# Weight loads in pairs of row pieces and a new instruction order, in four layers of local attention and gated products on one Trainium2 core

## The chip, the core and the metric

The kernel runs on one core of a Trainium2 chip. A core has five engines with a queue of instructions each: TensorE (PE in the profile; its weight loads, which overlap the products, are shown as PEld), VectorE (DVE), ScalarE (ACT), GpSimd (POOL) and SyncE (SP), which here only issues DMA transfers. An engine takes its instructions strictly in order, and each instruction may wait for semaphores that other engines or landed transfers raise. The metric is device time in microseconds; lower is better.

## What is computed

Two layers of attention and two of a gated product, in turn, over 2048 tokens of width 448, all in bfloat16, with the same weights both times:

```python
def _A_ref(x, wqkv, wo):
    H = 16; Dh = D // H
    W, dil = 8, 2
    qkv = (x @ wqkv)
    idx = pos[:, None] - off[None, :]
    logits = jnp.einsum("bhsd,bhswd->bhsw", q, kg) * scale
    attn = _softmax(logits, axis=-1)
    o = jnp.einsum("bhsw,bhswd->bhsd", attn, vg)
    return o @ wo
...
def _B_ref(x, w_gate, w_up, w_down):
    g = jnp.einsum("bsd,df->bsf", x, w_gate)
    u = jnp.einsum("bsd,df->bsf", x, w_up)
    h = g * u
    return jnp.einsum("bsf,fd->bsd", h, w_down)
...
x = x + _A_ref(_layernorm(x), A_wqkv, A_wo)
x = x + _B_ref(_layernorm(x), B_w_gate, B_w_up, B_w_down)
x = x + _A_ref(_layernorm(x), A_wqkv, A_wo)
x = x + _B_ref(_layernorm(x), B_w_gate, B_w_up, B_w_down)
```

Each query looks at 8 keys, 2 tokens apart, backwards. The inner width F of the gated product is 1792. Gate, up and down weights are 1.6 MB each.

## The kernel before

The program is a list of operations with dependencies; a list scheduler in the file (`Sched`, L134 to L522) puts them in order when the program is built, with estimated durations, and writes out one fixed instruction sequence for each engine. An operation's priority is a number for its job plus numbers for its kind (`PR`), for its place in the list (`XP`, some 1,300 entries) and for the job (`JP`). `HEAD_P`, `HOLD_A`, `HOLD_BA`, `HOLD_BB`, `A_CAP`, `B_CAP`, `ATT_P`, `LAND` and `LINE_H` also steer that choice alone. A different number gives a different order, and no other difference.

The tokens are cut into chunks of 256 or 512. A job "A20" is chunk 0 of layer 2, an attention layer; "B10" is chunk 0 of layer 1, a gated product. `SEQ` (L75) interleaves the jobs: `A00 A01 B10 A02 B11 A03 A04 B12 A20` and so on, so that attention work of one layer stands between gated products of another.

- A chunk of attention: normalization on VectorE and ScalarE (L761 to L782: statistics, logarithm and exponential for the root, xn), a transposed copy of xn in `xnTa` (by TensorE in the first layer, by a DMA transpose later), the query and key products (L534, evicted at L892), the value products (evicted at L957 and L984), a copy of some value rows through DRAM (`vt`, L901) that a DMA transpose brings back (L912).
- Attention runs in 9 groups of up to 240 tokens. A group has a score burst of up to 64 small products (L1015), two exponentials on ScalarE (L1024), two masks on VectorE (L1031), a value burst of 64 small products (L1049; AV1, AV2 and so on are the value bursts in the order of time), evictions (L1060, L1064), a shuffle, two passes on ScalarE for the reciprocal (L1074 to L1076), and the product oT (L1087). Then the output projection (L534, `wo_g`) and the add to x (L1104).
- A chunk of the gated product: xn of double width, its DMA transpose into `xnTb` (L785, L786), 14 units of 14 products with `WGU` (L534), each evicted by ScalarE (gate, L1140) and multiplied by VectorE (L1143) into `hT`, and the down products with `WD`.

A product with 64 rows of contraction takes half of the array; the two halves run at the same time, gate weights in partitions 0 to 63 and up weights in 64 to 127 of `WGU`. Small products of the bursts take an eighth each. Inside a burst the scheduler may place strips of a wide product (L537, 32 columns each), so that TensorE has work while its instructions come in.

All loads stand on SP's queue, in its order: x, qkv weights, `wo_g`, a row of ones for `vt`, then the weights of the gated product in six transfers of 784 KB, each waiting for the landing of the one in front: gate half 0, up half 0, gate half 1, up half 1, down half 0, down half 1 (L724 to L729). Behind them on the same queue are the copies to `vt`, the transposes from `vt` and the transposes into `xnTb`. A unit of the gate/up product waits for the gate and up halves that it reads (L1126), a down product for both down transfers.

## Time and profile before

| what | value |
|---|---|
| median of 3 runs | 394.8 us (394.6 to 395.0) |
| profiled execution | 395.59 us |
| its span, first to last instruction | 393.9 us |
| TensorE busy | 381.1 us, 97% |
| VectorE busy | 288.1 us, 73% |
| ScalarE busy | 208.3 us, 53% |
| granted TensorE clock, mean | 0.995 |
| HBM read and written | 8.54 MB, 2.71 MB |

The span runs from the first to the last instruction of the profiled execution; the time of that execution has some 1.7 us around it. A matmul's busy time is modelled to its end, so TensorE is busy also while a short product runs at the pace of its instructions. In stage rows the busy time of each engine stands with its number of instructions; the clock column is the share of full speed that TensorE was granted. In rows of groups a line of the kernel, the engine, the operation, the tiles written and read, the shapes and the count stand ahead of the bar, then the busy time and the mean of one in ns, then the idle time of the engine just before them and what ended it. SPq is SP's DMA queue: the length of a row is that of the issuing, not of the transfer.

### The profile page before, as it was taken

What the parts mean: (1) busy time and instruction counts of PE and PEld (TensorE: products, weight loads), DVE (VectorE), ACT (ScalarE), POOL (GpSimd) and SP (SyncE); (2) the same over time, 40 slices, a digit from 0 to 9 for tenths busy, and PEclk for the clock granted to TensorE, in tenths of its full rate; (3) what the DMA queues carried; (4) which work ended last, traced back from release to release, by engine and by line L of the source; (5) the groups of instructions that cost most, each with busy time, mean ns of one, the idle gap of its engine ahead of it and who ended that gap; (6) DMA issues with size and microseconds to landing.
All of it is one profiled execution on the core that took longest, in us unless ns stands there. A gap on an engine that the chain in (4) does not pass through costs nothing.

```text
span 393.9 us, 14839 instructions
## 1 busy us (share of the span) xinstructions
PE 381.1 (97%) x6577; PEld 214.8 (55%) x6577; DVE 288.1 (73%) x637; ACT 208.3 (53%) x392; POOL 8.8 (2%) x39
## 2 busy tenths in 40 slices
PE   8987879999999999999999999999999999999997
PEld 3644447755555454544575666755455445544764
DVE  6996787989995986598454997658978776766432
ACT  4887677757761665454445555445655543434410
POOL 7010000000000000000000000000000000000000
PEclk9999998999999999999999999999999999999999
DMA  8474663311331052301204022510314020304001
GB/s 277 128 154 91 165 147 48 60 38 24 41 63 25 17 77 52 37 2 36 44 17 60 3 41 51 82 33 27 54 26 73 25 47 3 96 1 49 2 25 48
DMA packets 54708, 22.53 MB, mean 57 GB/s; under 512 B 44837, under 2 KB 54645, under 8 KB 54645
## 3 DMA queue, kind: packets, MB, share of 16 engines
q1 hardware_dynamic: 54212, 21.07, 27.0%
q8 instruction: 52, 0.85, 0.9%
q10 hardware_dynamic: 432, 0.52, 0.5%
q14 instruction: 12, 0.09, 0.1%
HBM read 8.54 MB, written 2.71 MB: 29 GB/s over the span
## 4 chain that ended last, share of the span: by engine, by line
PE 86%; ACT 4%; DVE 4%; DMA 3%; issue 2%; SPq 1%
PE ps L534 77%; PE ps L537 3%; PE ps L1049 2%; PE ps L1015 2%; DMA x_sb<-in_A_x_dram 2%; PE ps L1155 1%; ACT qk L892 1%; ACT R_sb L1075 1%; SPq L627 1%; ACT E_sb L1024 1%; DMA xnTb<-xn_sb 1%; DVE hT L1143 1%; DVE x_sb L1104 1%; ACT R_sb L1076 1%; DVE st L761 1%
## 5 line engine op out<-in xcount | busy, mean ns | idle before, releaser
L534 PE MATMUL ps<-xnTb,WGU 64*128 64x512 bf16 (+1 forms) x1932 | 177.5, 335 | 2.3 <-DMA xnTb<-xn_sb 2.3
L534 PEld LDWEIGHTS ps<-xnTb,WGU 64*128 64x128 bf16 x1932 | 94.2, 94 | 76.4 <-issue 4.0
L1140 ACT ACTIVATE g_sb<-ps 128x512 bf16<-128x512 f32 (+1 forms) x140 | 71.5, 511 | 97.8 <-PE ps L534 79.1
L1143 DVE TENSOR_TENSOR hT<-g_sb,ps 128x512 bf16<-128x512 bf16 (+1 forms) x140 | 80.1, 577 | 47.8 <-ACT g_sb L1140 46.0
L534 PE MATMUL ps<-WD,hT 64*128 64x448 bf16 x760 | 77.6, 349 | 0.0
L534 PE MATMUL ps<-xnTa,WQK 64*128 64x512 bf16 (+1 forms) x492 | 53.5, 352 | 0.6 <-DVE hT L1143 0.4
L534 PEld LDWEIGHTS ps<-WD,hT 64*128 64x128 bf16 x760 | 35.8, 94 | 31.6
L1024 ACT ACTIVATE E_sb<-ps,shift_sb 128x1024 bf16<-128x1024 f32 (+1 forms) x36 | 36.8, 1071 | 20.5 <-PE ps L1015 20.4
L1104 DVE TENSOR_TENSOR x_sb<-x_sb,ps 128x448 bf16<-128x448 bf16 x62 | 36.0, 617 | 12.9 <-PE ps L534 12.7
L761 DVE BATCH_NORM_STATS2 st<-x_sb 128x6 f32<-128x448 bf16 x64 | 37.5, 615 | 0.1
L782 DVE TENSOR_SCALAR xn_sb<-x_sb,mv,rstd 128x896 bf16<-128x896 bf16 (+1 forms) x64 | 34.5, 570 | 3.2 <-ACT rstd L766 2.0
L534 PEld LDWEIGHTS ps<-xnTa,WQK 64*128 64x128 bf16 x492 | 24.2, 94 | 20.5 <-DVE hT L1143 0.8
L1031 DVE TENSOR_TENSOR E_sb<-E_sb,MK 128x1024 bf16<-128x1024 bf16 (+1 forms) x36 | 23.6, 664 | 11.1 <-ACT E_sb L1024 10.8
L534 PE MATMUL ps<-wo_g,oT 64*128 64x448 bf16 x252 | 29.2, 349 | 0.1
L892 ACT ACTIVATE qk<-ps 128x1024 bf16<-128x1024 f32 (+1 forms) x24 | 21.8, 917 | 12.8 <-PE ps L534 12.6
L1075 ACT ACTIVATE R_sb<-R_sb 128x480 f32<-128x480 f32 (+1 forms) x34 | 20.5, 603 | 8.0 <-DVE R_sb L1074 7.7
L1087 DVE TENSOR_TENSOR oT<-O_sb,R_sb 128x480 bf16<-128x480 f32 (+3 forms) x36 | 21.9, 628 | 2.7 <-ACT R_sb L1076 2.5
L1060 ACT ACTIVATE O_sb<-ps 128x448 f32<-128x448 f32 (+3 forms) x27 | 14.1, 553 | 18.0 <-PE ps L1049 17.9
L1074 DVE STREAM_SHUFFLE R_sb<-O_sb 128x480 f32<-128x480 f32 (+1 forms) x34 | 22.8, 696 | 0.0
L534 PE MATMUL ps<-WV,xnTa 64*128 64x336 bf16 (+3 forms) x242 | 22.5, 303 | 0.0
L892 DVE CAST qk<-ps 128x1024 bf16<-128x1024 f32 (+1 forms) x12 | 13.6, 1133 | 11.9 <-PE ps L534 11.9
L1076 ACT ACTIVATE R_sb<-R_sb 128x480 f32<-128x480 f32 (+1 forms) x34 | 19.8, 598 | 0.3
(66 smaller groups left out, 233.0 us busy)
## 6 DMA issues: line engine op xcount, KB each, us to landing
out_dram<-x_sb SPq DMA_DIRECT2D x15, 112.0 KB, 1.7
WGU<-in_B_w_gate_dram SPq DMA_DIRECT2D x2, 784.0 KB, 6.8
WGU<-in_B_w_up_dram SPq DMA_DIRECT2D x2, 784.0 KB, 6.6
WD<-in_B_w_down_dram SPq DMA_DIRECT2D x2, 784.0 KB, 4.8
x_sb<-in_A_x_dram SPq DMA_DIRECT2D x3, 448.0 KB, 6.0
vt<-qk SPq DMA_DIRECT2D x42, 16.0 KB
xnTb<-xn_sb SPq DMA_TRANSPOSE x32, 3.1
x_sb<-in_A_x_dram SPq DMA_DIRECT2D x2, 224.0 KB, 4.6
```

Source lines behind the costliest of these rows:

```text
L534: return lambda E: E.matmul(out(), lhs(), rhs(), start=start, stop=stop)
L761: sc.add("dve", one(lambda E, B=B: E.bn_stats(st6[:, B, :], x_sb[:, B, :]), ("bn", li, B)), 525.0, deps=[("x", li - 1, B)] + ([("xn", li - ...
L782: sc.add("dve", one(lambda E, B=B, dst=dst, src=src: E.tensor_scalar(dst, src, mv[:, B, 0:1], rstd[:, B:B + 1], ALU.subtract, ALU.mult), ( ...
L892: return E.activation(dst, src, ACT.Copy) if hasattr(E, "activation") else E.tensor_copy(dst, src)
L1024: return E.activation(E_sb[:, slot, 2 * hp:2 * hp + 2, 0:w], ps[:, b0:b0 + 2, 0:w], ACT.Exp, bias=shift_sb[:, 0:1], scale=SCALE)
L1031: return E.tensor_tensor(e, e, MK[:, kind, 0:nc].unsqueeze(1).unsqueeze(1).to_broadcast([128, 2, w // nc, nc]), ALU.min)
L1074: sc.add("dve", one(lambda E: E.stream_shuffle(R_sb[:, rs, 0:w], O_sb[:, os_, 0:w], [DH] * 32), ("Rs", li, qb)), dve_est(w) + 20.0, deps=[ ...
L1075: sc.add("act", one(lambda E: E.activation(R_sb[:, rs, 0:w], R_sb[:, rs, 0:w], ACT.Ln), ("Rl", li, qb)), act_est(w, False), deps=[("Rs", l ...
L1076: sc.add("act", one(lambda E: E.activation(R_sb[:, rs, 0:w], R_sb[:, rs, 0:w], ACT.Exp, scale=-1.0), ("R", li, qb)), act_est(w, False), de ...
L1104: sc.add("dve", one(lambda E: E.tensor_tensor(x_sb[:, B, :], x_sb[:, B, :], ps[:, bk[w], 0:D], ALU.add), ("x", li, B)), dve_est(D), deps=[ ...
L1140: sc.add("act", one(lambda E, gs=gs, bk=bk: E.activation(g_sb[:, gs, 0:nt], ps[:, bk[0], 0:nt], ACT.Copy), ("G", li, j, fc)), act_est(nt), ...
L1143: sc.add("dve", one(lambda E, gs=gs, bk=bk, fc=fc: E.tensor_tensor(hT[:, fc, hs, 0:nt], g_sb[:, gs, 0:nt], ps[:, bk[1], 0:nt], ALU.mult), ...
```

## The change

The loads of the gated product's weights are cut differently. For each half of F there are three pieces of rows (`KPARTS`: 2, 2 and 3 of the 7 row blocks of 64); the gate piece and the up piece are issued together, and the next pair waits for both to land. The down weights come in four pieces of 3, 4, 3 and 4 row blocks, each waiting for the piece in front. Pieces of one half share a semaphore, with a count for each (the scheduler's `mode`). A unit of the gate/up product waits for all three pieces of its half, a down product for all four. The transfer of ones waits for the four `wo` transfers as before.

All the numbers of the scheduler are new (`PR`, `XP`, `JP`, `HEAD_P`, the holds, `LAND`, `LINE_H`, `ATT_P`, `A_CAP`, `B_CAP`), so every engine's order is new. The instructions are the same but for the loads and the number of strips: 6565 products on TensorE instead of 6577. On SP's queue the first copies to `vt` stand between the fifth and the sixth pair, and two transposes into `xnTb` stand ahead of the first down piece; the fourth down piece stands behind a third one. On TensorE 999 products stand ahead of the first gate/up product instead of 935, among them the third value burst, and the first fourteen gate/up units have no burst between them.

```diff
-HEAD_P = (-2835.6, -2749.66, 4208.49, 2014.49, -243.09)
-HOLD_A = 5030.0
-HOLD_BA = 1290.0
-HOLD_BB = 620.0
+HEAD_P = (-7243.45, -6839.28, 6873.65, 2231.18, -2220.8)
+HOLD_A = 5940.0
+HOLD_BA = 13780.0
+HOLD_BB = 680.0
...
+KPARTS = ((0, 2), (2, 4), (4, 7))
...
-ATT_P = 6.0
-A_CAP = 6
-B_CAP = 8
+ATT_P = 3.0
+A_CAP = 5
+B_CAP = 6
...
-    LINE_H = 9300.0
+    LINE_H = 6500.0
...
-    def plain_dma(q, dst, src, key, sem, deps=(), lat=LOAD_L, prio=0.0, tmin=None):
+    def plain_dma(q, dst, src, key, sem, deps=(), lat=LOAD_L, prio=0.0, tmin=None, mode=0):
...
+    gate = [("wo", j) for j in range(4)]
     for n in range(2):
         f0, f1 = F // 2 * n, F // 2 * (n + 1)
-        plain_dma("sp", WGU[64:128, :, f0:f1], B_w_up[:, f0:f1].rearrange("(k p) f -> p k f", p=64), ("wu", n), f"d_wu{n}", deps=[("wg", n)], lat=LOAD_L + 784 / RATE, prio=-44)
-        plain_dma("sp", WGU[0:64, :, f0:f1], B_w_gate[:, f0:f1].rearrange("(k p) f -> p k f", p=64), ("wg", n), f"d_wg{n}", deps=[("wu", 0) if n else ("wo", 3)], lat=LOAD_L + 784 / RATE, prio=-44)
-    for n in range(2):
-        plain_dma("sp", WD[:, 7 * n:7 * n + 7, :], B_w_down[F // 2 * n:F // 2 * n + F // 2, :].rearrange("(c p) e -> p c e", p=128), ("wd", n), f"d_wd{n}", deps=[("wd", 0) if n else ("wu", 1)], lat=LOAD_L + 784 / RATE, prio=-44)
-    WDR = [("wd", 0), ("wd", 1)]
+        for i, (a, z) in enumerate(KPARTS):
+            for w, lo, src in (("wg", 0, B_w_gate), ("wu", 64, B_w_up)):
+                plain_dma("sp", WGU[lo:lo + 64, a:z, f0:f1], src[64 * a:64 * z, f0:f1].rearrange("(k p) f -> p k f", p=64), (w, n, i), f"d_{w}{n}", deps=gate, lat=LOAD_L + 224 * (z - a) / RATE, prio=-44, mode=i)
+            gate = [("wg", n, i), ("wu", n, i)]
+    for n in range(FC // 7 * 2):
+        a, z = 7 * n // 2, 7 * (n + 1) // 2
+        plain_dma("sp", WD[:, a:z, :], B_w_down[128 * a:128 * z, :].rearrange("(c p) e -> p c e", p=128), ("wd", n), f"d_wd{n // 2}", deps=gate, lat=LOAD_L + 112 * (z - a) / RATE, prio=-44, mode=n % 2)
+        gate = [("wd", n)]
+    WDR = [("wd", n) for n in range(4)]
...
-            return dict(bk=acq, out=out, n=nt, deps=[(w, n) for w in ("wg", "wu") for n in range(1 + (128 * fc + 128 > F // 2))],
+            return dict(bk=acq, out=out, n=nt, deps=[(w, n, i) for w in ("wg", "wu") for n in range(1 + (128 * fc + 128 > F // 2)) for i in range(len(KPARTS))],
```

More of the change, by code (lines that the diff above doesn't have):

```diff
@@ L61 @@
-JP = {'A20': -697.04, 'B32': -598.99, 'B34': -1387.93, 'A22': 1516.07, 'B13': 3108.07, 'A21': -1307.14, 'B12': -64.59, 'A02': 125.15, 'A03': 770.84, 'B30': 3086.52, 'B31': -1192.52, 'B10': -1995.52, 'B11': -915.69, 'A23': -3947.09, 'A04': -1459.04, 'B33': -501.93, 'A01': -1029.7, 'B14': -665.97, 'A00': 1187.84}
+PR = {'Qz': 1078.85, 'AV': -4851.85, 'rstd': -1339.07, 'bn': 4568.65, 'N': -1817.78, 'Gps': 8610.65, 'Tps': -31.38, 'H': -4889.6, 'S': 2643.48, 'VT': 544.99, 'Ex': 596.45, 'G': -2837.24, 'xn': -3500.95, 'QK': 2639.1, 'Ddps': 940.66, 'V': 567.07, 'x': -8.65, 'lnv': 5266.82, 'Oc': 2625.17, 'Oa': 3443.2, 'R': -727.31, 'VVps': -3592.23, 'Yps': -11164.33, 'PW': 3164.05, 'T': -1396.37, 'mv': -2211.6, 'Rs': 1799.38, 'Rl': -488.18, 'QKps': 1399.61, 'E': 778.94, 'wqk': 1537.92, 'wqp': 1028.96}
@@ L62 @@
+JP = {'A20': -25.69, 'B32': -196.33, 'B34': -5191.89, 'A22': -98.13, 'B13': 6648.45, 'A21': -2562.96, 'B12': 1135.93, 'A02': 1939.91, 'A03': 1924.97, 'B30': 4558.29, 'B31': -653.55, 'B10': -3350.57, 'B11': -1722.9, 'A23': -7569.63, 'A04': -2325.27, 'B33': 4017.0, 'A01': -2467.87, 'B14': -3725.84, 'A00': -900.45}
 LOAD_L = 2000.0
-LAND = {"x0": 3800.0, "x0h": 6250.0, "x1": 7450.0, "x2": 10100.0, "x3": 12350.0, "stg0": 3700.0, "stg2": 4900.0, "stg1": 5050.0, "stg3": 5650.0, "wv": 8850.0, "stv": 10550.0}
+LAND = {"x0": 3850.0, "x0h": 6700.0, "x1": 7950.0, "x2": 10600.0, "x3": 12050.0, "stg0": 3500.0, "stg2": 4800.0, "stg1": 5100.0, "stg3": 5650.0, "wv": 9300.0, "stv": 11000.0}
@@ L624, in act_table_load @@
         return E.add_instruction(atl)
-    def plain_dma(q, dst, src, key, sem, deps=(), lat=LOAD_L, prio=0.0, tmin=None):
-        sc.add(q, one(lambda E: E.dma_start(dst, src), key), {"sp": 520.0, "act": 500.0, "pool": 1000.0}[q], deps=deps, dma=sem, mode=0, lat=lat, land=LAND.get(sem[2:], 0.0), prio=prio, tmin=tmin)
+    def plain_dma(q, dst, src, key, sem, deps=(), lat=LOAD_L, prio=0.0, tmin=None, mode=0):
+        sc.add(q, one(lambda E: E.dma_start(dst, src), key), {"sp": 520.0, "act": 500.0, "pool": 1000.0}[q], deps=deps, dma=sem, mode=mode, lat=lat, land=LAND.get(sem[2:], 0.0), prio=prio, tmin=tmin)
     CH_ROWS = [0, 128, 192, 320]
@@ L718, in build @@
     ones_src = ones32[0:32, :].unsqueeze(1).to_broadcast([32, 16, 128])
-    plain_dma("sp", ones_dst, ones_src, ("vones",), "d_one", deps=["c_ones", ("wo", 3)], lat=8000.0, prio=-44.5)
+    plain_dma("sp", ones_dst, ones_src, ("vones",), "d_one", deps=["c_ones"] + [("wo", j) for j in range(4)], lat=4000.0, prio=-44.5)
     for j in range(4):
@@ L722, in build @@
         src = A_wo.rearrange("(c j e) d -> j e c d", c=4, j=4, e=DH)[j]
-        plain_dma("sp", dst, src, ("wo", j), "d_wo", deps=["c_wo", ("x", -1, 11)], lat=LOAD_L + 98 / RATE, prio=-45)
+        plain_dma("sp", dst, src, ("wo", j), "d_wo", deps=["c_wo", ("x", -1, 11)], lat=3600.0, prio=-45)
+    gate = [("wo", j) for j in range(4)]
     for n in range(2):
         f0, f1 = F // 2 * n, F // 2 * (n + 1)
-        plain_dma("sp", WGU[64:128, :, f0:f1], B_w_up[:, f0:f1].rearrange("(k p) f -> p k f", p=64), ("wu", n), f"d_wu{n}", deps=[("wg", n)], lat=LOAD_L + 784 / RATE, prio=-44)
-        plain_dma("sp", WGU[0:64, :, f0:f1], B_w_gate[:, f0:f1].rearrange("(k p) f -> p k f", p=64), ("wg", n), f"d_wg{n}", deps=[("wu", 0) if n else ("wo", 3)], lat=LOAD_L + 784 / RATE, prio=-44)
-    for n in range(2):
-        plain_dma("sp", WD[:, 7 * n:7 * n + 7, :], B_w_down[F // 2 * n:F // 2 * n + F // 2, :].rearrange("(c p) e -> p c e", p=128), ("wd", n), f"d_wd{n}", deps=[("wd", 0) if n else ("wu", 1)], lat=LOAD_L + 784 / RATE, prio=-44)
-    WDR = [("wd", 0), ("wd", 1)]
+        for i, (a, z) in enumerate(KPARTS):
[7 more added lines that the diff above has]
+    WDR = [("wd", n) for n in range(4)]
     WO = [("wo", j) for j in range(4)]
```

3 lines of the change are left out of this document (1 added, 2 removed).

## The prediction

> **What bounds the kernel now.** I read the page first, then the stages, then TensorE's waits, then the queue that issues the loads.
>
> ```profile
> span 393.9 us, 14839 instructions
> ...
> q8 instruction: 52, 0.85, 0.9%
> ```
>
> The profiled execution took 395.59 us: the span and 1.7 us around it. The runs shown have a median of 394.8, so this execution is 0.8 above them; I add my sum to the median.
>
> Stages (length, then busy us and instruction counts of PE, PEld, DVE, ACT, POOL, then granted clock, DMA share, GB/s):
>
> ```profile
> 0.00:58.36 58.36, 48.66 (x935) 27.27 (x936) 48.03 (x127) 41.35 (x77) 8.75 (x39) 1.00 0.64 162
> 25.80:32.70 6.90, 5.23 (x127) 2.68 (x128) 5.08 (x13) 4.88 (x6) 0.00 (x0) 1.00 0.66 128
> 32.70:39.19 6.49, 6.08 (x127) 3.86 (x127) 4.96 (x10) 5.60 (x11) 0.00 (x0) 1.00 0.57 118
> 58.36:76.31 17.95, 17.95 (x468) 13.75 (x470) 14.09 (x38) 12.73 (x30) 0.00 (x0) 0.90 0.34 49
> 58.98:62.39 3.41, 3.41 (x112) 2.35 (x110) 0.79 (x3) 1.68 (x4) 0.00 (x0) 0.50 0.17 29
> 76.31:391.30 314.99, 314.46 (x5178) 173.81 (x5173) 225.64 (x473) 154.19 (x286) 0.00 (x0) 1.00 0.22 38
> ```
>
> From 76.31 us on TensorE is busy 314.46 of 314.99 us while VectorE has 28% to spare: an order can gain next to nothing there. Ahead of it lie 9.7 us of idle TensorE (58.36 less 48.66) and a stretch of 3.41 us at clock 0.50, which costs half its length, **1.7 us**. All that this change can win is in these first 76 us. TensorE's waits:
>
> ```profile
> PE ps L1049 <- issue: 3.3, 2, 1.7
> PE ps L534 <- DMA xnTb<-xn_sb: 2.3, 1, 2.3
> ...
> PE ps L1015 <- issue: 1.0, 2, 0.6
> ```
>
> "Issue" means that TensorE waited for nothing the profile shows. These four stalls, **4.3 us**, end at 25.80, 32.70, 39.19 and 45.84, and the stage rows say what they are: exactly 127 matmuls lie between one end and the next. The page has 52 packets in the instruction queue for 6577 matmuls and as many weight loads: one packet holds some 253 instructions, the 127 matmuls with their loads. TensorE stands at the end of a piece of its program and waits for the next. The load queue gives the beat (start, length of the issue):
>
> ```profile
> 17.45 0.71 SPq L627 DMA_DIRECT2D WGU<-in_B_w_gate_dram  x1
> 24.23 0.59 SPq L627 DMA_DIRECT2D WGU<-in_B_w_up_dram  x1
> ...
> 49.39 4.33 SPq L901 DMA_DIRECT2D vt<-qk  x12
> 53.76 2.68 SPq L785 DMA_TRANSPOSE xnTb<-xn_sb  x2
> ```
>
> The weight loads follow each other every 6.8 us (17.45 to 24.23), and the stalls end every 6.9, 6.5 and 6.7 us. I read it so: an instruction packet stands behind the whole weight transfer in flight. The last two rows explain the wait of 2.3 us: the transposes that the first gate/up product reads stand on the same queue, behind all six weight loads and twelve copies.
>
> ```profile
> 45.84 0.70 PE ps L1049 x59
> ...
> 55.16 2.96 DMA xnTb<-xn_sb
> ```
>
> So the second attention group's value products (AV2) end at 46.5 us, the first gate/up product starts at 58.36.
>
> **The change part by part.** *Loads.* Six transfers of 784 KB become twelve of 224 or 336 KB in six pairs, then four down pieces of 336 or 448 KB, in the same rows and bytes.
>
> ```profile
> out_dram<-x_sb SPq DMA_DIRECT2D x15, 112.0 KB, 1.7
> WGU<-in_B_w_gate_dram SPq DMA_DIRECT2D x2, 784.0 KB, 6.8
> WGU<-in_B_w_up_dram SPq DMA_DIRECT2D x2, 784.0 KB, 6.6
> WD<-in_B_w_down_dram SPq DMA_DIRECT2D x2, 784.0 KB, 4.8
> ```
>
> No row shows a pair. Between 112 KB in 1.7 us and 784 KB in 6.8 us, in proportion, a pair of 448 KB takes 4.2 us and one of 672 KB 5.9; by the down row's 4.8 us it is 3.3 and 4.3; at worst each step costs 6.8. I take the dearer proportion, since both halves write 64 partitions as the gate does: six pairs 28.6 us, landed at 17.45 + 28.6, with a delay behind seven copies **at about 46.6 us**. Down pieces come to 2.7 and 3.3 us. Ten more issues of about 0.6 us put 6 us on SP's queue. Behind its waits stand the copies to vt, the value transposes and the xnTb transposes; in the new order two xnTb transposes stand ahead of all down pieces, and the fourth down piece stands behind a transpose that waits for VectorE.
>
> *Instruction stalls.* A packet now waits for a pair's stream, at most 5.9 us and mostly under 4.2, with a gap after each. The bounds are 4.3 us gained and none. What they covered comes forward: the attention chain. Its prices:
>
> ```profile
> L1024 ACT ACTIVATE E_sb<-ps,shift_sb 128x1024 bf16<-128x1024 f32 x32 | 34.0, 1112 | 20.5 <-PE ps L1015 20.4
> ...
> L1143 DVE TENSOR_TENSOR hT<-g_sb,ps 128x256 bf16<-128x256 bf16 x56 | 23.1, 418 | 18.4 <-ACT g_sb L1140 17.9 <-PE ps L534 0.5
> L782 DVE TENSOR_SCALAR xn_sb<-x_sb,mv,rstd 128x896 bf16<-128x896 bf16 x32 | 22.9, 735 | 2.3 <-ACT rstd L766 1.4 <-DMA xnTa<-xn_sb 0.9
> L1031 DVE TENSOR_TENSOR E_sb<-E_sb,MK 128x1024 bf16<-128x1024 bf16 x32 | 21.9, 690 | 11.1 <-ACT E_sb L1024 10.8
> L1140 ACT ACTIVATE g_sb<-ps 128x256 bf16<-128x256 f32 x56 | 21.4, 384 | 34.8 <-PE ps L534 24.3 <-DVE hT L1143 9.5 <-DVE mv L763 0.8
> L1074 DVE STREAM_SHUFFLE R_sb<-O_sb 128x480 f32<-128x480 f32 x32 | 21.4, 695 | 0.0
> L1087 DVE TENSOR_TENSOR oT<-O_sb,R_sb 128x480 bf16<-128x480 f32 x30 | 19.3, 655 | 2.7 <-ACT R_sb L1076 2.5
> L1075 ACT ACTIVATE R_sb<-R_sb 128x480 f32<-128x480 f32 x32 | 19.2, 601 | 5.9 <-DVE R_sb L1074 5.5
> L1076 ACT ACTIVATE R_sb<-R_sb 128x480 f32<-128x480 f32 x32 | 18.6, 596 | 0.3
> L892 ACT ACTIVATE qk<-ps 128x1024 bf16<-128x1024 f32 x18 | 18.4, 1025 | 11.7 <-PE ps L534 11.5
> ```
>
> In the new order the second half of AV1 waits for two exponentials (2.2 us), a copy out of PSUM half an eviction long (0.6) and an eviction (1.0) after the second score burst. That burst waits for the same vector work as before and ends just after 25.80 again: 29.8, and AV1, 1.1 us long, ends at 31.0. Eleven vector operations (three shuffles, two oT products, an eviction, two v copies, three small ones) then take 7.2 us to the third score burst; that burst, a reciprocal, an eviction, two exponentials and a mask take 4.2, AV2 itself 1.1. **AV2 ends at 43.5 us, 3.0 earlier**, at the same amount of TensorE work done. So 1.3 of the 4.3 us goes back to ACT and VectorE.
>
> *The wait for xnTb.* After AV2 the new order puts the fourth score burst and AV3 ahead of the first gate/up product. VectorE reaches the second xn at AV2 + 4.5; SP then has three copies (0.36 each by the row of twelve) and the transpose (1.34, and 3.0 to its landing), which is down at AV2 + 9.3. TensorE gets to that product only at AV2 + 11.6, because AV3 waits for a mask that ACT's two reciprocals (four passes of 0.6), two evictions and two exponentials precede. Before it was 11.9. The wait for DMA is hidden, a wait of 1.1 us for the mask takes its place; with 0.2 us more streaming and one burst more done by then this is **0.9 us won**. The product starts at 55.1.
>
> *Clock.* The half-clock stage starts 0.6 us after the idle of 2.3 us and takes 1.7 us. The two waits of 1.6 and 1.7 us had none behind them. I count it as caused by the longer idle and gone with it: **1.7 us**; the bounds are 0 and 1.7.
> [...]
>
> *First down projection.* The spacing of TensorE's work:
>
> ```profile
> 75.56 0.94 PE L534 MATMUL ps<-xnTb,WGU 64*128 64x256 bf16 x14
> 76.31 1.50 PE L534 MATMUL ps<-WD,hT 64*128 64x448 bf16 x14
> ```
>
> A unit of 14 matmuls of 256 columns takes 0.75 us; other widths I take in proportion. By the count of the order, streaming up to the first down product is 56.9 us before and 55.4 after. The new order runs all fourteen gate/up units without a score or value burst between them. VectorE must put out 14 products (5.9 us), four adds and four statistics (5.2 at the 0.65 of the other 448 to 480 wide operations), three xn (2.2), two shuffles and two oT (2.7): 16.0 us, of which 1 us falls ahead of the stretch, against 13.2 us of streaming. I walk to 15.0 us from the first gate/up product to the first down product; before it was 17.95 with 1.7 of half clock, 14.9 of streaming and three bursts: 0.1 of waiting. **1.7 us lost** (bounds 0.5 and 2.5). The first down product is then at 70.1 us.
>
> *Down weights.* The fourth piece is issued after the transpose of the third xn, at about 65.2, and lands by 68.9: 1.2 us to spare. So nothing.
>
> *The rest.* Streaming is the same, 361.4 us in all. A burst costs 0.4 us beside its streaming (76.31 to the end: 315 us for 304.5 of streaming and 25 bursts); there are 33 runs of bursts instead of 34: **0.4 us won**. Constants, estimates and semaphore modes make no instruction of their own. The order behind 76 us I count at 0, bounds 1 won and 2 lost: nothing spare covers it.
>
> Sum: -3.0 - 0.9 - 1.7 + 1.7 - 0.4 = **-4.3 us, 390.5 us**.
>
> **The rivals.** [...] 0.12. [...]
> *Instruction packets still wait*: pairs fill the queue as a single load did, 1.0 instead of 3.0 is won: 392.5. For: two requests may meet a 672 KB pair. 0.13.
> *The lead is given back* to VectorE behind the first down product: about 394.4. For: it is busy 14.09 of 17.95 us there; against: its 28% idle after 76.31. 0.10.
> *Slower*: a step costs 6.7 us whatever its size. Six pairs end at 17.45 + 40.2 = 57.7, just in time for the fourth gate/up unit, which needs the second half; four down pieces of 4.8 end at 76.9, 6.8 us after TensorE wants them, and an idle that long brings 1.7 of half clock: 390.5 + 8.5 = 399.0. It decides once the last piece lands over 2.6 us late. For: ten landings in a row instead of six, the last behind a transpose; against: 112 KB land in 1.7 us. The change would then not do what it says. 0.11.
>
> **How the numbers follow.** The forecast holds 0.50 (389.5 to 391.8), a gain beyond it, down to 388.8 where the gate/up run loses nothing, 0.04. A measurement tells 0.2%, 0.8 us, from no change. Faster: 0.50 + 0.04 + 0.12 + 0.13 and 0.04 of the third rival, 0.83; same 0.06; slower 0.11. The range 388.8 to 393.9 takes in the first two rivals and most of the third.
>
> **What would show it.** Right: TensorE's issue waits under 1.5 us in all; no wait for xnTb; no 0.50 clock between 50 and 70 us; first gate/up product near 55, first down product near 70; copies of the gate loads on SP's queue every 4 to 6 us. Wrong: a TensorE wait for WGU or WD, a half-clock stage, or a sum of TensorE waits behind 76 us above 2 us.

## The result, and the profile after

The changed kernel takes 390.69 us (median of 15 runs, 388.63 to 394.44) beside 394.84 for the kernel before (15 runs, 393.19 to 396.09) on the same chip: a ratio of 0.9899, 95% interval 0.9873 to 0.9925. The forecast was 390.5. Its profiled execution took 391.56 us with a span of 389.6. All lines of the kernel from the first table on stand a little lower: L534 is now L535, L1015 is L1021, L1024 is L1030, L1049 is L1055, L1143 is L1149, L785 is L791.

TensorE's waits in the changed kernel (total, times, longest, in us):

```profile
PE ps L535 <- DMA WD<-in_B_w_down_dram: 1.4, 1, 1.4
PE ps L697 <- DVE eps_sb L658: 1.3, 1, 1.3
PE ps L1021 <- issue: 1.2, 1, 1.2
PE ps L802 <- DVE WQK L713: 0.7, 1, 0.7
PE ps L1021 <- ACT xnTa L812: 0.6, 1, 0.6
PE ps L535 <- ACT E_sb L1030: 0.3, 1, 0.3
```

The wait of 2.3 us for xnTb is gone, and of 4.3 us of issue stalls one of 1.2 us is left. A wait of 1.4 us for the down weights is new. The same stages as before, then the half-clock stage (length, busy us and counts of PE, PEld, DVE, ACT, POOL, granted clock, DMA share, GB/s):

```profile
0.00:55.62 55.62, 51.00 (x999) 28.39 (x1000) 46.83 (x125) 41.08 (x79) 7.83 (x37) 0.97 0.60 147
55.62:70.48 14.86, 13.45 (x227) 12.04 (x228) 14.16 (x36) 9.15 (x25) 0.00 (x0) 1.00 0.55 134
...
70.48:387.00 316.52, 316.26 (x5340) 174.25 (x5340) 225.59 (x477) 158.81 (x290) 0.00 (x0) 1.00 0.22 39
26.64:30.05 3.41, 3.41 (x34) 2.11 (x30) 2.02 (x4) 2.30 (x4) 0.00 (x0) 0.50 0.83 186
```

TensorE's idle time ahead of the first gate/up product falls from 9.70 to 4.62 us, the stretch to the first down product has 1.41 us of idle where it had none, and what follows has 0.26 instead of 0.53. That is 3.94 us less idle. Busy time up to the end of these stages falls by 0.36. Together 4.30 us, which is all of the shorter span. The half-clock stage is still there. It has moved from 58.98 to 26.64.

The chain of waits (start, length, what) shows the milestones:

```profile
43.72 0.09 PE ps L1055 x19
43.80 4.79 PE ps L535 x52
48.59 0.22 PE ps L1021 x16
48.81 1.22 issue
...
55.62 8.60 PE ps L535 x148
...
66.43 3.96 DMA WD<-in_B_w_down_dram
...
70.48 1.50 PE ps L535 x14
```

| milestone, us | before | forecast | after |
|---|---|---|---|
| AV2 ends | 46.5 | 43.5 | 43.8 |
| first gate/up product | 58.36 | 55.1 | 55.62 |
| first down product | 76.31 | 70.1 | 70.48 |

The milestones move from one execution to the next. The first matmuls of 512 columns start 0.43 us apart until the clock is full and 0.215 us apart from there on, and that moment comes at 4.36 us in the profile of before, at 6.16 in this one and at 4.89 in a second profile of the changed kernel, which has its milestones at 43.0, 53.70 and 68.66. By the spacing, the 1.8 us between the first two cost the changed kernel some 0.9 us in this comparison (an estimate); the clock column does not count that stretch.

The queue that issues the loads (start, length of the issue):

```profile
16.37 0.70 SPq L628 DMA_DIRECT2D WGU<-in_B_w_gate_dram  x1
...
21.03 0.60 SPq L628 DMA_DIRECT2D WGU<-in_B_w_gate_dram  x1
...
65.10 1.28 SPq L791 DMA_TRANSPOSE xnTb<-xn_sb  x1
66.43 0.58 SPq L628 DMA_DIRECT2D WD<-in_B_w_down_dram  x1
```

The first two pairs, 448 KB each, are 4.66 us apart, where single loads of 784 KB were 6.8 apart: pieces do land in less time, as assumed. All six pairs take longer than forecast: the last one lands at 49.61 and not at about 46.6, which costs nothing, since the first gate/up product starts at 55.62. The fourth down piece is issued at 66.43, behind a transpose for which VectorE had to finish, and TensorE wants it at 69.1.

### The profile page after: what moved, and what is told of

Its sections match the earlier page's. It is cut to its first block, busy times and chain, and to the rows that moved or that the text cites. A ratio compares the mean times of both kernels' runs of the same rounds, so it can differ in the third digit from the quotient of the medians.

```text
span 389.6 us, 14816 instructions
## 1 busy us (share of the span) xinstructions
PE 380.8 (98%) x6565; PEld 214.7 (55%) x6565; DVE 287.0 (74%) x638; ACT 209.0 (54%) x393; POOL 7.8 (2%) x37
## 4 chain that ended last, share of the span: by engine, by line
PE 93%; ACT 3%; DMA 1%; issue 1%; DVE 1%; SPq 0%; ACTq 0%
PE ps L535 82%; PE ps L538 3%; PE ps L1055 2%; PE ps L1021 2%; PE ps L697 2%; ACT E_sb L1030 1%; PE ps L1161 1%; DMA WD<-in_B_w_down_dram 1%; ACT xnTa L812 1%; ACT qk L898 1%; ACT g_sb L1146 0%; ACT xnTa L809 0%; DVE x_sb L1110 0%; PE ps L802 0%; DVE hT L1149 0%
## 5 line engine op out<-in xcount | busy, mean ns | idle before, releaser
L535 PE MATMUL ps<-xnTb,WGU 64*128 64x512 bf16 (+1 forms) x1908 | 174.4, 332 | 0.2
L535 PEld LDWEIGHTS ps<-xnTb,WGU 64*128 64x128 bf16 x1908 | 92.6, 94 | 67.8 <-issue 1.1
L1149 DVE TENSOR_TENSOR hT<-g_sb,ps 128x512 bf16<-128x512 bf16 (+1 forms) x140 | 79.6, 576 | 43.1 <-ACT g_sb L1146 40.7
L535 PE MATMUL ps<-WD,hT 64*128 64x448 bf16 x778 | 78.6, 349 | 1.5 <-DMA WD<-in_B_w_down_dram 1.4
L535 PEld LDWEIGHTS ps<-WD,hT 64*128 64x128 bf16 x778 | 36.9, 94 | 36.0 <-issue 1.7
L535 PE MATMUL ps<-xnTa,WQK 64*128 64x512 bf16 (+1 forms) x492 | 55.2, 360 | 0.5 <-ACT E_sb L1030 0.3
L1030 ACT ACTIVATE E_sb<-ps,shift_sb 128x1024 bf16<-128x1024 f32 (+1 forms) x36 | 36.8, 1073 | 24.5 <-PE ps L1021 24.4
L535 PEld LDWEIGHTS ps<-xnTa,WQK 64*128 64x128 bf16 x492 | 23.9, 96 | 22.2 <-issue 1.5
L898 ACT ACTIVATE qk<-ps 128x1024 bf16<-128x1024 f32 (+1 forms) x26 | 24.6, 956 | 11.3 <-PE ps L535 11.2
L535 PE MATMUL ps<-wo_g,oT 64*128 64x448 bf16 x256 | 29.1, 349 | 0.1
L535 PE MATMUL ps<-WV,xnTa 64*128 64x336 bf16 (+3 forms) x248 | 23.1, 304 | 0.0
L1009 DVE TENSOR_SCALAR Qz<-qk,qmask 128x960 bf16<-128x960 bf16 (+1 forms) x36 | 14.7, 451 | 9.2 <-PE ps L1021 8.0
L535 PEld LDWEIGHTS ps<-wo_g,oT 64*128 64x128 bf16 x256 | 12.4, 94 | 12.4 <-DVE oT L1093 0.9
```

The lines of the kernel that those rows point to most:

```text
L535: return lambda E: E.matmul(out(), lhs(), rhs(), start=start, stop=stop)
L898: return E.activation(dst, src, ACT.Copy) if hasattr(E, "activation") else E.tensor_copy(dst, src)
L1030: return E.activation(E_sb[:, slot, 2 * hp:2 * hp + 2, 0:w], ps[:, b0:b0 + 2, 0:w], ACT.Exp, bias=shift_sb[:, 0:1], scale=SCALE)
L1149: sc.add("dve", one(lambda E, gs=gs, bk=bk, fc=fc: E.tensor_tensor(hT[:, fc, hs, 0:nt], g_sb[:, gs, 0:nt], ps[:, bk[1], 0:nt], ALU.mult), ...
```

## The experiments

The questions were: is it the pieces or the order that takes the stalls away; is a packet of instructions really behind the transfer in flight; what brings the half-clock stage; and what the late down piece costs. In the diffs that move something on SP's queue, `SPQ` is that queue after the scheduler has run, so that no other engine's order changes. The last four runs were made on one chip, with a median of 394.31 us for the kernel before; the first four beside 394.66, the second four beside 395.16.

### The new order with whole loads

```diff
+            o.ins = [(lambda E, n=n, f0=f0, f1=f1, lo=lo, src=src: E.dma_start(WGU[lo:lo + 64, :, f0:f1], src[:, f0:f1].rearrange("(k p) f -> p k f", p=64)), (w, n, 0))]
+            o.deps = [("wg", n, 0)] if w == "wu" else [("wu", 0, 0)] if n else [("wo", j) for j in range(4)]
+            for i in (1, 2):
+                SPQ.pop(at((w, n, i)))
...
+        o.ins = [(lambda E, n=n: E.dma_start(WD[:, 7 * n:7 * n + 7, :], B_w_down[F // 2 * n:F // 2 * n + F // 2, :].rearrange("(c p) e -> p c e", p=128)), ("wd", 2 * n))]
+        SPQ.pop(at(("wd", 2 * n + 1)))
```

> The new order with the six whole loads of before, each on the landing of the one in front. Theory (an instruction packet stands behind the weight transfer in flight, so small pieces took the stalls away): TensorE's issue waits come back, 3 to 4 us in the first 55 us instead of 1.2, at a beat of 6.5 to 6.9 us; the wait of 1.4 us for WD goes, since the second down load is issued where piece three was (57 to 61 us) and lands by 66. Sum 390.7 + 2.5 - 1.4 = 391.8 us (391 to 393). Rival (the order alone took the stalls away): issue waits stay near 1.2 us, WD wait gone, 389.3 us.

390.35 us (4 runs, 389.72 to 392.12), ratio 0.9904, 0.9877 to 0.9931: as fast as the changed kernel. Its chain and its load queue:

```profile
24.92 0.41 issue
25.33 0.24 PE ps L1021 x2
...
31.23 0.92 issue
32.16 0.23 PE ps L1055 x9
...
43.66 1.50 issue
45.17 0.27 PE ps L1055 x20
```

```profile
23.77 0.60 SPq L1245 DMA_DIRECT2D WGU<-in_B_w_up_dram  x1
30.39 0.60 SPq L1245 DMA_DIRECT2D WGU<-in_B_w_gate_dram  x1
...
59.93 0.41 SPq L1251 DMA_DIRECT2D WD<-in_B_w_down_dram  x1
```

With whole loads three stalls of 2.8 us in all are back, each ending some 1.6 to 1.8 us after a load gave way to the next (25.33 after 23.77, 32.16 after 30.39; the third, 45.17, stands 1.6 us behind the landing of the fourth load at 43.58). The trace also has the instruction packets themselves, on queue q8, 16 KB each. Those that TensorE waits for here end at 24.07, 30.55 and 43.88, each 0.2 to 0.3 us behind the landing of a load, and TensorE goes on 1.3 to 1.6 us after each. In the profile of the kernel before such packets end at 24.50, 31.09, 37.66 and 44.50, 0.1 to 0.3 us behind the landings of the first four loads, and TensorE goes on 1.3 to 1.6 us after each. The theory of the stalls holds. But the time does not rise by the 2.5 less 1.4 us expected: this order starts its last down load at 59.93, and there is no wait for WD at all. The stalls came out smaller than the expected 3 to 4, and the two sums cancel.

The same two kernels once more, side by side:

> The new order with the six whole loads, again. If the pieces gain in issue stalls what they give back in the wait for WD: within 0.6 us of the changed kernel, with issue stalls of 2.4 to 2.8 us and no wait for WD. Rival (the pieces are worth a gain of their own that the first run missed): 1 us or more above the changed kernel.

> The changed kernel again, beside the next two on one chip. 390.7 us, waits of 1.2 us for instructions and 1.4 us for WD.

Whole loads 390.21 us (6 runs, ratio 0.9879, 0.9853 to 0.9906), the changed kernel 390.16 (6 runs, 0.9881, 0.9855 to 0.9908), with 2.8 us of issue stalls and no wait for WD in the first and 0.2 of stalls and 1.5 of WD in the second. **In the new order the cutting of the loads shows no gain (each ratio is known to some 1 us either way); the whole 4.1 us come with the order.** The first profile with whole loads says how. Its first gate/up product starts at 56.44, and TensorE is idle for 5.95 us ahead of it instead of 9.70: the issue stalls are 1.5 us less than in the kernel before, and the wait of 2.25 us for xnTb is gone.

### Uncut pairs

```diff
+            o.ins = [(lambda E, n=n, f0=f0, f1=f1, lo=lo, src=src: E.dma_start(WGU[lo:lo + 64, :, f0:f1], src[:, f0:f1].rearrange("(k p) f -> p k f", p=64)), (w, n, 0))]
+            for i in (1, 2):
+                SPQ.pop(at((w, n, i)))
```

> The changed kernel with gate and up of each half issued together but uncut: two pairs of 1568 KB in flight instead of six of 448 and 672. Theory (packets wait for what is in flight): a pair streams for some 10 to 13 us, so a packet that is asked for early in it comes up to 8 us late; issue waits of 4 to 10 us in all, time 393 to 398 us. Rival (issuing both halves together is what helped, not the size in flight): issue waits near 1.2 us, 390.7 us.

393.13 us (10 runs, ratio 0.9969, 0.9948 to 0.999). Load queue, then chain:

```profile
18.43 0.62 SPq L1245 DMA_DIRECT2D WGU<-in_B_w_up_dram  x1
28.94 0.59 SPq L1245 DMA_DIRECT2D WGU<-in_B_w_gate_dram  x1
```

```profile
24.09 0.66 PE ps L1021 x50
24.76 4.10 issue
28.85 0.24 PE ps L1021 x2
```

The stall starts where it did with whole loads (24.92 there) but lasts 4.10 us instead of 0.41. That it ends where the next pair is issued, 28.85 against 28.94, looks like a wait for the whole pair, but the packet's own record speaks against it. From 25.7 to 27.2 us the DMA queues (packets, MB, share of the 16 engines' time) show the packet among those of the load:

```profile
q1 hardware_dynamic: 134, 0.22, 79.2%
q8 instruction: 1, 0.02, 5.7%
```

It runs from 25.80 to 27.17, behind the gate load, which landed at 24.89, and ahead of the end of the up load, which landed at 28.88; TensorE goes on 1.7 us after it. In the four stalls of the kernel before that was 1.3 to 1.6 us, and in the one of the changed kernel 1.5 (the packet ended at 48.50, TensorE goes on at 50.03). With whole loads the same packet ended 3.1 us earlier, at 24.07. So with 1568 KB in flight TensorE stood longer than with 784 KB (4.10 us for 0.41), but the packet did not wait for all of it. The second pair hit nothing that waited.

### The old order with the new pieces

```diff
+    for key, fn, total in ((("wg", 0), s_g0, 48), (("wu", 0), s_u0, 48), (("wg", 1), s_g1, 48), (("wu", 1), s_u1, 48), (("wd", 0), s_d0, 32), (("wd", 1), s_d1, 32)):
+        SPQ[i] = ([o], [(o, fn)])
```

Each `s_` function waits for the piece in front and issues one pair (the fourth place three pairs, a down place two pieces).

> The old order on all engines, with the pieces in the old six places of SP's queue (pairs in the gate and up places, two down pieces in each down place). Theory: issue waits shrink from 4.3 us to 1 to 2 us, but ten landings instead of five stand in front of the copies to vt and the xnTb transposes, so these come 4 to 8 us later than at 53.76 us and the wait for xnTb grows from 2.3 to some 7 us: 396 to 400 us, slower than before. Rival (loads alone bring the gain): 391 to 392 us.

405.71 us (4 runs, ratio 1.0298, 1.0264 to 1.0333). A wait of TensorE and the rows of the queue behind it:

```profile
PE ps L535 <- DMA xnTb<-xn_sb: 10.2, 1, 10.2
```

```profile
54.68 3.33 SPq L1246 DMA_DIRECT2D WD<-in_B_w_down_dram  x2
58.05 4.25 SPq L902 DMA_DIRECT2D vt<-qk  x12
62.35 2.68 SPq L786 DMA_TRANSPOSE xnTb<-xn_sb  x2
```

The direction was expected, the size was not (7 us of wait, 396 to 400 us), and the issue stalls are 3.4 us, not 1 to 2. The transposes come 8.6 us later than at 53.76, and the clock is halved from 61.9 to 72.2 us, around and behind that idle. In the second form the down places were moved behind the transposes, the first of them by

```diff
+    move(("wd", 0), ("T", 1, 1))
+    move(("wd", 1), ("VT", 0, 7))
```

> As the run with the old order and the new pieces, but the first two down pieces stand behind the first two xnTb transposes and the other two behind a later value transpose. Theory: issue waits 1 to 2 us instead of 4.3, and the wait for xnTb shrinks under 1 us as the transposes no longer wait for down weights; ACT and VectorE take back about 1.3 us: 391 to 392.5 us. Rival (only the whole new order can use the pieces, since the old one's queues wait elsewhere): 394 to 395 us.

396.27 us (4 runs, ratio 1.0048, 1.0031 to 1.0064), slower than before.

```profile
PE ps L535 <- DMA xnTb<-xn_sb: 3.2, 1, 3.2
PE ps L1016 <- issue: 1.5, 1, 1.5
```

```profile
48.47 1.34 SPq L786 DMA_TRANSPOSE xnTb<-xn_sb  x1
49.91 3.39 SPq L1246 DMA_DIRECT2D WD<-in_B_w_down_dram  x2
53.35 1.22 SPq L786 DMA_TRANSPOSE xnTb<-xn_sb  x1
```

The issue stalls ahead of the first gate/up product are 1.5 us; in the first form, with the same load queue up to 46 us, they were 3.4. The packets came alike: the second of them ended at 32.20 there and at 31.91 here. But here TensorE ran at half clock from 26.58 to 29.99, so it wanted that packet at 33.22 and not at 31.85, and did not have to wait. A smaller sum of stalls is thus not by itself a gain. The edit put the down pieces between the two transposes and not behind both, so the second one again left the queue at 53.35, and the product waits as before. So the second transpose's place on SP's queue keeps the first gate/up product at 57.78, for 58.36 before, though AV2 ends some 1.8 us earlier. The old order with both transposes ahead of all down pieces was not run.

### One move on the queue of the kernel before

```diff
+    es = [SPQ.pop(at(("T", 1, b))) for b in (0, 1)]
+    j = at(("wd", 1))
+    SPQ[j:j] = es
```

> The kernel before with the two xnTb transposes of 53.76 us moved ahead of the second down load on SP's queue, nothing else. Common to both theories: the wait of 2.3 us for xnTb shrinks by 1.5 to 2.3 us. Theory C of the prediction (that idle causes the half-clock stage): the stage at 59 us goes too, 394.8 - 2.0 - 1.7 = 391.1 us and a clock of 1.00 in all runs. Rival (the stage is free of the program): 392.8 us, and the clock varies between runs as in the kernel before.

397.2 us (12 runs, 394.8 to 399.25, ratio 1.0048, 1.0027 to 1.0069): slower, against both theories. The queue and the chain:

```profile
48.91 2.67 SPq L785 DMA_TRANSPOSE xnTb<-xn_sb  x2
51.62 1.88 SPq L627 DMA_DIRECT2D WD<-in_B_w_down_dram  x1
53.54 4.29 SPq L901 DMA_DIRECT2D vt<-qk  x12
```

```profile
76.00 3.33 PE ps L534 x36
79.33 3.00 DMA xnTb<-xn_sb
```

The wait at 55 us went, and the first down product starts at 72.09 instead of 76.31. But the transposes now keep the second down load and the twelve copies to vt back, the transposes from vt that follow end at 77.93 instead of 75.73, and the next two into xnTb, behind those on the queue, start at 77.98 instead of 76.68. A value burst at 79 us, which holds strips that read xnTb, waits 3.1 us, and a half-clock stage follows at 83.23. The wait moved and got longer, and what had been won is given back: the profiled execution takes 396.04 us, beside 395.59 before. Why the median lies another 1.2 us higher is not shown. This one move, without the work of the other engines, cannot use the earlier transpose.

### The clock

> The kernel before, unchanged, to read the granted clock of each execution. If the half-clock stage is tied to the idle of 2.3 us ahead of it, it stands at the same place (59 to 62 us) in the profile and the clock is 0.995 to 0.996 in every run; if it runs free of the program, the profile shows it at another place or not at all, and the clock varies from run to run between 1.00 and 0.99. Time 394.8 us.

394.76 us (12 runs). Its profile has the half-clock stage where it was (58.86 us), but over the 59 runs of the kernel before whose clock is on record, 14 have a mean of 1.00 (median 394.0 us), 34 of 0.995 or 0.996 (395.0) and 11 less (394.9). So one stage goes with about **1.0 us** by these medians, though the runs with two are no slower than those with one, and in the changed kernel the difference is 0.5 us (390.1 for 9 runs, 390.6 for 10). A stage is there in most runs, not in all.

The stage lasts 3.41 us in these profiles, and in two others two or three times that: 6.83 with uncut pairs (24.97 to 31.80), 10.24 in the old order with pieces (61.92 to 72.16). In the kernel before the clock is full from 4.36 us on and halved at 58.98, 54.61 us later; in the changed kernel it is full from 6.16 on and halved at 26.64, 20.48 us later. These are 16 and 6 times 3.413, so windows of that length, laid back to back from the moment at which the clock is full, end where these stages begin. The windows ahead of the stages, and some that had none behind them (first the kernel before: no stage follows its first row, one follows its second, at 58.98):

```profile
21.43:24.84 3.41, 2.09 (x99) 1.47 (x95) 3.29 (x12) 3.41 (x6) 1.22 (x6) 1.00 0.45 82
...
55.56:58.97 3.41, 1.16 (x18) 0.75 (x16) 2.87 (x6) 0.87 (x1) 0.00 (x0) 1.00 0.61 115
```

The changed kernel (the stage at 26.64 follows), and the second profile of the kernel with the fourth down piece early, which is described below (none follows):

```profile
23.22:26.64 3.42, 1.88 (x94) 1.41 (x96) 3.42 (x12) 3.42 (x6) 0.57 (x3) 1.00 0.34 96
```

```profile
23.90:27.31 3.41, 2.22 (x100) 1.63 (x100) 3.41 (x12) 3.41 (x7) 0.23 (x2) 1.00 0.27 72
```

What goes with a stage is the share of the window ahead of it in which TensorE is busy: 34% and 55% are followed by one here, 61% and 65% are not. Of all the windows in the profiles of the kernel before and the changed one, those of 34%, 36% (at the end) and 55% are followed by one, and those of 59% or more are not. In other profiles windows of 30% (the kernel before again), 43% (the sixth pair later), 48% and 52% (whole loads again), 54% (uncut pairs) and 56% (the changed kernel again) are followed by one. At 61% both occur: that window of the kernel before had no stage behind it, and 61% at the same place, in the run with one move on its queue, had one at 25.21, where twelve products take 2.48 us that took 1.40 before. No run sets the busy share alone, so this is read from the windows, not tested. No long single idle stands ahead of the stage at 26.64: the waits of 0.7, 0.6 and 0.3 us for WQK, xnTa and E_sb lie in or beside the window that ends there. Counted from the full clock, the windows start at another moment in each execution (4.36 us in one profile of the kernel before, 4.25 in the other), so the same idle time can fall into one window in one run and into two in the next. That the clock follows such windows is the author's reading; no run shows it by itself.

### The late down piece

```diff
+    move(("wd", 3), ("wd", 2))
+    opof(("wd", 3)).deps = [("wd", 1)]
```

> The changed kernel with the fourth down piece issued right behind the third, both on the landing of the second. Theory (the piece is late because it stands behind a transpose that waits for VectorE): the wait of 1.4 us for WD goes and the first down product starts near 69.1 us: 389.3 us. Rival (the gate/up stretch is bound by VectorE, as the prediction had it): the wait for WD is replaced by waits for hT, 390.5 us.

389.65 us (4 runs, 389.46 to 390.12, ratio 0.9868, 0.9849 to 0.9888). Once more, on the chip of the last four runs:

> The changed kernel with only the fourth down piece issued with the third, again. If the wait for WD is what it pays for: 1.0 to 1.4 us below the changed kernel on the same chip (389.3 to 389.7 us). Rival (the difference of 1.0 us seen first was scatter between runs): within 0.4 us of it.

388.75 us (6 runs, 387.61 to 389.73, ratio 0.9845, 0.9819 to 0.9871), 1.4 below the changed kernel beside it. The stretch from the first gate/up product to the end of the first down unit, which holds 1.5 us of down products:

```profile
53.06:68.03 14.97, 14.97 (x257) 11.65 (x261) 14.16 (x36) 9.11 (x25) 0.00 (x0) 1.00 0.58 145
```

There is no wait for WD, and none for VectorE: TensorE is busy all 14.97 us. The rival, a gate/up stretch bound by VectorE, falls. The edit changes two things, the place on the queue and the landing that the piece waits for. In the changed kernel the third piece landed at 65.21, so the place alone made the fourth 1.2 us later, issued at 66.43; the two were not tried apart.

Two attempts at the stall of 1.2 us that was left, behind the sixth pair. Issuing that pair later:

```diff
+    es = [SPQ.pop(at((w, 1, 2))) for w in ("wg", "wu")]
+    j = next(i for i, (got, _) in enumerate(SPQ) if got[0].ins[0][1] == ("VT", 0, 8)) + 1
+    SPQ[j:j] = es
```

> The changed kernel with the fourth down piece early, as in the other run, and the sixth gate/up pair (672 KB) issued behind the two value transposes instead of ahead of them. Theory (the one issue stall left, 1.2 us ending at 50.03, is a packet behind that pair): the stall goes, or moves to another place with less than 0.5 us: 388.3 us. Rival (transposes and the pair now meet, xnTb or the second half of F comes late): a new wait for xnTb or WGU of 1 us or more, 389.3 us or above.

390.9 us (6 runs, 388.66 to 393.22, ratio 0.9898, 0.9865 to 0.9931), 1.25 above the run with the down piece alone, a difference that is not clear of the scatter. The stall shrank from 0.9 to 0.6 us, and the profile has the wait that the rival named:

```profile
PE ps L535 <- DMA xnTb<-xn_sb: 1.4, 1, 1.4
...
PE ps L1055 <- issue: 0.6, 2, 0.4
```

Making the sixth pair smaller:

```diff
+        for i, (a, z) in enumerate(((0, 3), (3, 5), (5, 7))):
+                opof((w, n, i)).ins = [(lambda E, a=a, z=z, f0=f0, f1=f1, lo=lo, src=src: E.dma_start(WGU[lo:lo + 64, a:z, f0:f1], src[64 * a:64 * z, f0:f1].rearrange("(k p) f -> p k f", p=64)), (w, n, i))]
```

> The changed kernel with the fourth down piece early, and the pieces of each half cut 3, 2, 2 instead of 2, 2, 3 row blocks, so that the sixth pair is 448 KB and not 672 KB. Theory (the stall of 0.9 to 1.2 us that is left in the fourth score burst is a packet behind the sixth pair): it shrinks under 0.5 us, 0.5 to 0.9 us below the run that only has the fourth down piece early. Rival (the large pairs, now first and fourth, catch another packet): the stall moves to one of the bursts near 25, 31, 37 or 43 us with about the same length, and the time stays within 0.4 us of that run.

388.74 us (6 runs, 388.35 to 389.19, ratio 0.9847, 0.9824 to 0.987), with no issue stall in the profile. But the kernel without this edit, run beside it, has none in its profile either and takes 388.75: its stall of 0.9 us is there in one execution and not in the next. In the one TensorE began the packet ahead of the stall at 42.68, after the sixth pair was issued at 41.44, and the next packet ended at 47.74; in the other it began it at 41.81, just ahead of the pair at 41.89, and the next one ended at 44.04. Whether the smaller last pair is worth anything stays open.

## Why the prediction was right, and where it was not

The time came within 0.2 us. The milestones came within 0.5 us in the first profile and 0.5 to 1.4 us ahead of the forecast in the second, so that their closeness is in part luck of the execution. Half of the terms behind them did not come true, and of the prediction's signs of being wrong two appeared: a wait for WD and a half-clock stage.

*Instruction stalls* (3.0 won by AV2): measured 2.7, and 3.5 in the second profile. The mechanism is shown three ways: the uncut pairs made a stall of 4.10 us, the whole loads brought three stalls back, each just behind a landing, and the packets' own records stand behind the loads. In the old order a cut by the pieces is not shown: the sums are 3.4 and 1.5 us with pieces, and 4.3, 3.4 (again) and 1.3 (with one move on the queue) with whole loads, ahead of the first gate/up product. What the prediction did not see is that the new order alone, with whole loads, has 2.8 us of these stalls and not 4.3. "1.3 of the 4.3 us goes back to ACT and VectorE" is not borne out: no wait for a mask or an exponential grew over 0.3 us. Up to AV2 TensorE is idle 4.2 us less but busy 1.5 us longer, at the same amount of streaming: the clock is full 1.8 us later in this execution, and the half-clock stage, now at 26.64, stands ahead of AV2.

*The wait for xnTb* (0.9 won): the wait is hidden, as predicted, by the fourth score burst and AV3 put ahead of the product. The 1.1 us for the mask in its place did not come (0.2 in the runs without an issue stall); an issue stall of 1.2 us stood there. The runs with the transposes on other places of SP's queue, in the old order, show that such a move alone did not do it.

*Clock* (1.7 won): **this step failed.** The stage does go from 58.98, as the idle of 2.3 us goes, but one stands at 26.64 behind a window of 55%, and eight of the nine profiled executions of that order have a stage (mean clock 0.991 to 0.996, 1.00 in the ninth); in the old order a window of 61% had one behind it in one run and none in another. In the 21 runs of the changed kernel 9 have none, against 14 of 59 before, at 1.0 us for a stage: the saving is some 0.2 us in the mean and nothing between the two profiled executions. No run shows what the 0.12 in the sum of the chances rests on; the runs showed a stage in 12 of those 21, for 0.5 us by the medians.

*First down projection* (1.7 lost to VectorE): the size was right, 14.86 us to the first down product for 15.0, **and the cause was wrong**. The runs with the down piece early show 14.97 us less 1.5 of down products, 13.5 us, near the 13.2 of pure streaming: VectorE, with 14.16 us of work beside it, costs nothing there. *Down weights* (1.2 us to spare) failed as well, by 2.6: the fourth piece was issued 1.2 us later than predicted and took 3.96 us, and the 1.4 us of idle are all its own. The prediction named the place, behind a transpose that waits for VectorE, and gave it a chance in the slower rival. Its two errors cancel: 15.0 us from the measured start at 55.62 end at 70.6, where the piece landed at 70.39, so that a stretch as slow as assumed would just have hidden it.

*The rest* held where it can be seen: TensorE behind the first down product is idle for 0.26 us. The 0.4 us for one burst less is not shown by itself; busy time falls by 0.36, with the later full clock in it.

So the sum was right by luck: the idle ahead of the first gate/up product fell by 5.1 us where terms of 3.9 stood, and the clock gave nothing where 1.7 stood. And the diff's first half, the pieces, is not what pays: they win up to 2.6 us in stalls and give 1.4 to 1.5 back at the last down piece, and the times are level with whole loads (390.16 and 390.21). With that piece issued beside the third the new loads are worth 1.5 us, and the kernel takes 388.75, a ratio of 0.9845 to the one before.

## What to carry to other kernels

An idle engine that "waits for nothing" may be waiting for its own instructions: look whether its stalls lie a fixed count of instructions apart (127 matmuls here), end soon after a large transfer lands (1.6 to 1.9 us in the kernel before) and follow a packet on the instruction queue (by 1.3 to 1.6 us), and keep what is in flight small while engines are short of work (4.10 us of stall with uncut pairs, 1.2 and 0.2 with cut ones). On a queue in strict order a weight load must not stand behind something that waits for an engine, unless its landing has that wait to spare (the fourth down piece cost 1.4 us); and a single move on such a queue can send the wait elsewhere (2.3 us ahead of 58.36 became 3.1 us at 79). When a forecast comes out right, test its terms one by one: here two wrong causes cancelled.

## What the hardware showed that was not expected

The clock was halved for 3.41 us, or two or three times that: from 58.98 us on in the profile of the kernel before, behind 3.41 us in which TensorE was busy 34%, and from 26.64 on in that of the changed kernel, behind 55%. Neither of these two profiles has a stage behind 59% or more; another had one behind 61%. The same kernel has a stage in one run and none in the next (14 of 59 runs of the kernel before have a mean clock of 1.00), for about 1.0 us of 395 by the medians. At the start the clock became full at 4.36 us in the profile of the kernel before and at 6.16 in that of the changed kernel, and until then matmuls of 512 columns started 0.43 us apart instead of 0.215.

A pair of 1568 KB in flight held TensorE up for 4.10 us, until 1.7 us after its packet of instructions had come in among that pair; pairs of 448 and 672 KB for 0 to 1.2 us in the new order, differently from one execution to the next of the same kernel.
